# Seven block products for a sequence transform, with the feature transform behind them

## The chip, the cores and the metric

One core of a Trainium2 chip runs the kernel. The metric is the device time of one execution in microseconds (us); the kernel before takes 1925.48 us, the median of three runs.

The core's engines are TensorE (PE in the profile; PEld is its loading of weights), VectorE (DVE), ScalarE (ACT) and GpSimd (POOL); SP issues most transfers. TensorE writes into eight PSUM banks of 128 x 512 floats; TensorE's operands come from SBUF.

## The reference, cut to what matters

Four layers on an x of 2048 rows (the sequence) by 512 columns (the features): a spectral layer, an attention layer, and the same two again.

```
def _A_ref(x, dft_seq_re, dft_seq_im, dft_hid_re, dft_hid_im):
    a = jnp.einsum("bsd,ed->bse", x, dft_hid_re)
    b = jnp.einsum("bsd,ed->bse", x, dft_hid_im)
    return jnp.einsum("ts,bse->bte", dft_seq_re, a) - jnp.einsum("ts,bse->bte", dft_seq_im, b)

x = x + _A_ref(_layernorm(x), ...)      # spectral: both transforms, real part
x = x + _B_ref(_layernorm(x), ...)      # segmented attention with a memory, 32 heads, 4 segments
x = x + _A_ref(_layernorm(x), ...)
x = x + _B_ref(_layernorm(x), ...)
```

All is float32. The sequence matrices are 2048 x 2048, the feature matrices 512 x 512. Either transform may be done first; both kernels do the sequence first.

## The kernel before

Each float32 operand of a large product is split into a hi part (rounded to fp32r, TensorE's fast float format) and a lo part (the rest): ScalarE makes hi (L83), VectorE or GpSimd makes lo = source - hi (L85). `matmul3` (L91, matmuls at L71 of the wrapper) then issues three matmuls, hi hi, hi lo and lo hi.

A spectral layer (`place_spectral`) has these parts. `normalise(i)` loads one of 16 row tiles (128 x 512), takes its statistics, makes xn (L143) and splits it into `xh[i]`: hi on ScalarE, lo on GpSimd. `load_c(p, pc)` loads two row tiles' worth of the sequence matrix for a block of 512 output rows and splits it into chi and clo, 1024 wide. `contract(p)`, p from 0 to 7 (four column blocks `tcn` of 512 rows, real and imaginary), runs over the 16 row tiles: four PSUM banks u, one for each 128 features, 12 matmuls a tile. At the end of a pass the four banks are split into ut. `hidden(tcn)` multiplies them with the feature matrices wdt, eight steps of three matmuls for each of 16 row tiles of output y, and `finish` adds the residual xr (L148, VectorE) and stores the row. The hidden steps of three column blocks lie between the steps of later passes; those of the fourth lie one to a slot at the start of the attention.

The attention layer (`place_attention`) transposes the normalised rows, makes q, k and v (pqk, pvv), writes pieces of q and k to DRAM and reads them back as stacks, takes row maxima of the scores (`natural_max`, L418 on VectorE), the scores again for the softmax (sT, L483 and L484 on ScalarE), the product with the values into `pv_bank`, and the output projection (po).

The order is written out by hand. `place(order, generator, slots)` puts each step of a generator in a numbered slot; the slots are then run through in order, within a slot by `order`. Matmuls keep this order on TensorE; the other engines' order is planned from it, each engine then running its list in order. The sequence transform takes two slots for a row tile, 256 slots in all; the attention begins (`b1`, `b2`) at slot 286 of its spectral layer, and its first projections, stacks and maxima lie up to 60 slots ahead of that.

Buffers: tag `w` has 16 pairs (xh, later the attention's weights), `chi` and `clo` three each, `craw` two, `ut` and `wd` eight each. PSUM has seven rotating banks and `pv_bank` for good.

Of the kernel before, what the change touches and what calls it, by code (L numbers as in the profile page):

```python
# [37 lines left out]
MROWS = 3  # L38
MCOPIES = 5
VW = DH + 1  # L40
CP = 2
URGENT = 150


@with_exitstack
def spectral_infini_kernel(
# [58 lines left out]
    def pair(name, tag, bufs, dtype=F32R):  # L105
        return sb.tile([P, 2, 512], dtype, name=name, tag=tag, bufs=bufs)
# [10 lines left out]
        split(w[:, 0], w[:, 1], raw)  # L117
        yield

    def row_stats(xt):  # L120
        st = sb.tile([P, 6], F32, name="st", bufs=2)
        V.bn_stats(st, xt)
        mv = sb.tile([P, 2], F32, name="mv", bufs=3)
        V.bn_aggr(mv, st)
        ve = sb.tile([P, 1], F32, name="ve", bufs=3)
        V.tensor_scalar_add(ve, mv[:, 1:2], EPS)  # L126
        r = sb.tile([P, 1], F32, name="r", bufs=3)
        G.tensor_tensor(out=r, in0=ve, in1=half_neg, op=ALU.pow)  # L128
        return mv, ve, r
# [6 lines left out]
    def layernorm(xt, mv, ve, r):  # L136
        t = sb.tile([P, 1], F32, name="rt", bufs=2)
        V.scalar_tensor_tensor(t, r, r, ve, op0=ALU.mult, op1=ALU.mult)
        V.tensor_scalar(t, t, -0.5, 1.5, op0=ALU.mult, op1=ALU.add)  # L139
        rr = sb.tile([P, 1], F32, name="rr", bufs=2)  # L140
        V.tensor_mul(rr, r, t)
        xn = sb.tile([P, D], F32, name="xn", bufs=2)
        V.tensor_scalar(xn, xt, mv[:, 0:1], rr, op0=ALU.subtract, op1=ALU.mult)  # L143
        return xn
# [20 lines left out]
    def run_from(t, n, step=1):  # L165
        return range(t, t + n * step, step)

    def place_spectral(x_in, x_out, t0, ln_at, resident):
        xh, cs, wdt, u = {}, {}, {}, {}
        NP = 2 * TC  # L170

        EARLY = 12 if t0 else 0
        PRE = 4 if t0 else 0
        pre = []

        def kt(p, i):
            return t0 + 2 * (p * NT + i) - (4 if p == 0 and i < EARLY else 0)

        def preload():
            pre.append(sb.tile([P, PRE, CP, 512], F32, name="cpre", tag="xT", bufs=1))  # L180
            for pc in range(PRE):
                for c in range(CP):
                    nc.sync.dma_start(pre[0][:, pc, c], ct[0, 0, pc, :, c])
                    yield

        def normalise(i):
            leads = i == 0 and t0 == 0
            xt = None if i in LAST and t0 else load_rows(x_in[i])
            yield
            xt = resident[i] if xt is None else xt  # L190
            with behind_first(0 < i < 3):
                stats = row_stats(xt)
            yield
            xn = layernorm(xt, *stats)
# [6 lines left out]
        def load_c(p, pc):  # L201
            if p == 0 and pc < PRE:
                raw = pre[0][:, pc]
            else:
                raw = pair("craw", "craw", 2, F32)
                nc.sync.dma_start(raw, ct[p % 2, p // 2, pc])
            yield
            hi, lo = pair("chi", "chi", 3), pair("clo", "clo", 3)
            with behind_first(p == 0 and pc == 0):
                split(hi, lo, raw)  # L210
            cs[p, pc] = (hi, lo)
            yield

        def contract(p):
            us = [bank(f"u{d}") for d in range(DT)]
            for i in range(NT):
                cp = cs[p, i // CP]
                for d in range(DT):
                    matmul3(
                        us[d],  # L220
                        lambda h: xh[i][:, h, d * P : (d + 1) * P],
                        lambda h: cp[h][:, i % CP],
                        i == 0,
                        i == NT - 1,
                    )
                if i < NT - 1:
                    yield
            for d in range(DT):
                ut = pair("ut", "ut", 8)
                split(ut[:, 0], ut[:, 1], us[d], 1.0 if p % 2 == 0 else -1.0)  # L230
                u[p, d] = ut
            yield

        def hidden(tcn):
            for tt in range(LT):
                ps = bank("y")
                xr = load_rows(x_in[tcn * LT + tt], "xr")
                for c in range(2):
                    for d in range(DT):
                        ut, w = u[2 * tcn + c, d], wdt[c, d]  # L240
                        matmul3(
                            ps,
                            lambda h: ut[:, h, tt * P : (tt + 1) * P],
                            lambda h: w[:, h, :],
                            (c, d) == (0, 0),
                            (c, d) == (1, DT - 1),
                        )
                        if (c, d) != (1, DT - 1):
                            yield
                finish(ps, xr, x_out, tcn * LT + tt)  # L250
                yield

        for i in range(NT):
            t = ln_at(i)
            place(3, normalise(i), [t, t, t] if i == 0 and t0 == 0 else [t - (8 if i < 12 else 4), t - 3, t])
        if PRE:
            place(2.5, preload(), [kt(0, 0) - 46 + 10 * k + c for k in range(PRE) for c in (0, 2)])
        for p in range(NP):
            for pc in range(NT // CP):
                t = kt(p, pc * CP)  # L260
                place(3, load_c(p, pc), [t - 10, t - (2 if p == 0 and pc < PRE else 4)])
            place(2, contract(p), [kt(p, i) for i in range(NT)])
        for k in range(2 * DT):
            c, d = k // DT, k % DT
            t = kt(1, k)
            place(3, load_split(wdt, (c, d), wd[c, d], "wdt", "wd", 8), [t - 3, t])
        nh = 2 * DT * LT
        for tcn in range(TC):
            if tcn < TC - 1:
                at = [kt(2 * tcn + 2, 2) + 3 * k // 4 for k in range(nh)]  # L270
            else:
                at = run_from(kt(NP, 0), nh)
            place(4, hidden(tcn), at)

    def place_attention(x_in, x_out, t0, w_at, out_at, resident):
        ws, xT, vt, o_nat, state, scr, phi, stacks, maxima, outs = ({} for _ in range(10))
        k_stacks = []

        def prep(s, i):
            xt = load_rows(x_in[s * LT + i])  # L280
# [181 lines left out]
        def softmax_values(s, g, u):  # L462
# [83 lines left out]
                ev(h // 2, third)  # L546

            def last():
                pb = pv_bank
# [159 lines left out]
        def outproj_split(s, i):  # L709
# [23 lines left out]
            finish(ps, xr, x_out, s * LT + i, tag="wd", bufs=8)  # L733
            yield

        def alloc_out(s):
            o_nat[s] = [pair("onat", "wd", 8, F32) for _ in range(LT // 2)]
            yield
# [20 lines left out]
        for k in range(4 * DT):  # L759
            n, d = "qkvo"[k // DT], k % DT  # L760
            src = rows((wq, wk, wv, wo)[k // DT], d)
            place(3, load_split(ws, (n, d), src, f"w{n}", "w", 16), [w_at(k) - 3, w_at(k)])
        for n in range(NSEG * USEG):
# [49 lines left out]
    ]  # L813

    resident = {}
    LB, LEAD = NSEG * NG * (HG // HU) * 10, 46
    a1 = 0
    b1 = a1 + 240 + LEAD
    a2 = b1 + LB + 1
    b2 = a2 + 240 + LEAD  # L820

    def w_at(b):
        return lambda k: b - 52 + 2 * k if k < 12 else b - 14 + 2 * (k - 12)

    place_spectral(x_tiles, mids[0], a1, lambda i: a1 - 6 + 2 * i - (30 if i == 0 else 0), resident)
    place_attention(
        mids[0], mids[1], b1, w_at(b1), lambda k: b1 + LB + 8 + k // 2, resident
    )
# [88 lines left out]
```

## Time and profile before

| | |
|---|---|
| median of three runs | 1925.48 us (1923.19 to 1926.77) |
| profiled execution | 1927.09 us, of which the span of the profile is 1925.3 |
| TensorE busy | 1841.9 us, 96% |
| VectorE, ScalarE, GpSimd busy | 57%, 50%, 27% |
| mean transfer rate | 120 GB/s |
| matmuls of the sequence transforms (u) | 3072, of 10528 |
| first matmul; last of the first transform; last y of it | 9.4; 440; 492 us |
| first and last u of the second transform; last y of it | 963; 1397; 1448 us |

Rows of groups give the code line, the engine, the operation, the tile written and those read, the shape, the count, then busy us and mean ns of one, then the idle time before them and what ended it. A tile's own rows give least, median and greatest duration in ns instead, then the first and the last start. Tables of stretches give for each stretch its length, then busy us (and instructions) of PE, PEld, DVE, ACT and POOL, the granted TensorE clock, the share of the DMA engines and GB/s. Time lines give the start, the duration, and what ran; equal neighbours are merged with a count. Instructions of one engine are pipelined, so one can start about 0.1 us before its predecessor's end.

### The profile page before, as it was taken

How to read it: one execution, taken by the hardware profiler on the slowest of the kernel's cores; microseconds unless marked ns; L12 is line 12 of the kernel's file. 1: busy time of each engine (PE TensorE's matmuls, PEld its weight loads, DVE VectorE, ACT ScalarE, POOL GpSimd, SP SyncE). 2: the span in 40 equal slices, each digit the busy share in tenths (PEclk: the TensorE clock that was granted, in tenths of full speed). 3: DMA queues.
4: the chain of work that ended last, by engine and by line, in shares of the span. 5: the costliest groups of instructions: out<-in, count | busy, mean ns of one | idle time of the engine just before them, and what ended most of it. 6: DMA issues, size and time to landing. Idle time of an engine off the chain costs nothing. (4 is left out here: it accounts for less than half of the span.)

```text
span 1925.3 us, 30850 instructions
## 1 busy us (share of the span) xinstructions
PE 1841.9 (96%) x10528; PEld 1330.9 (69%) x10528; DVE 1092.2 (57%) x3665; ACT 961.1 (50%) x2026; POOL 515.1 (27%) x854
## 2 busy tenths in 40 slices
PE   7899999999989999998899999999999999999998
PEld 5788888887656666665478888888875566666654
DVE  8522222254777977878744222222557778777674
ACT  3321212132677778687733122121427877777775
POOL 5100000003443435355420000000134434444442
PEclk9999999999999999999999999999999999999999
DMA  5523222345443433435224322222454324344331
GB/s 177 162 88 110 92 95 98 104 151 159 134 125 109 152 114 128 138 117 166 73 98 142 99 98 94 95 97 94 158 170 138 127 93 151 114 130 139 110 123 45
DMA packets 122542, 231.41 MB, mean 120 GB/s; under 512 B 14352, under 2 KB 63504, under 8 KB 122384
## 3 DMA queue, kind: packets, MB, share of 16 engines
q1 hardware_dynamic: 119120, 228.65, 36.8%
q8 instruction: 83, 1.36, 0.3%
q10 hardware_dynamic: 3264, 0.79, 0.2%
q14 instruction: 75, 0.61, 0.1%
HBM read 161.50 MB, written 67.11 MB: 119 GB/s over the span
## 5 line engine op out<-in xcount | busy, mean ns | idle before, releaser
L71 PE MATMUL u<-chi,xh 128*128 128x512 f32 x2048 | 650.2, 391 | 15.1 <-ACT chi L83 9.4
L418 DVE CUSTOM_DVE_ANT_0 junk<-nat,mask 128x512 bf16<-128x512 f32 (+3 forms) x1024 | 496.4, 485 | 176.0 <-PE nat L71 156.1
L71 PEld LDWEIGHTS u<-chi,xh 128*128 128x128 f32 x2048 | 385.7, 188 | 97.5 <-ACT chi L83 9.4
L71 PE MATMUL u<-clo,xh 128*128 128x512 f32 x1024 | 400.0, 391 | 3.1 <-DVE clo L85 3.1
L83 ACT ACTIVATE chi<-craw 128x1024 fp32r<-128x1024 f32 x124 | 131.3, 1059 | 530.0 <-PE u L71 512.7
L85 DVE TENSOR_TENSOR clo<-craw,chi 128x1024 fp32r<-128x1024 f32 x124 | 153.2, 1236 | 421.2 <-ACT chi L83 420.7
L484 ACT ACTIVATE pT<-sT 128x512 f32<-128x512 f32 x640 | 369.2, 599 | 15.4 <-ACT sT L483 3.0
L487 POOL TENSOR_SCALAR_AFFINE_SELECT pT<-pT 128x256 f32<-128x256 f32 (+1 forms) x448 | 197.8, 455 | 416.4 <-ACT pT L484 346.5
L71 PE MATMUL sT<-stkq,stkk 99*128 99x256 bf16 (+3 forms) x1024 | 247.7, 305 | 14.1 <-DVE mx L418 4.6
L71 PE MATMUL nat<-stkk,stkq 96*128 96x512 bf16 (+3 forms) x1024 | 245.3, 300 | 15.5 <-DVE mx L418 12.4
L128 POOL TENSOR_TENSOR r<-ve,half_neg 128x1 f32<-128x1 f32 x64 | 39.1, 611 | 815.9 <-DVE ve L126 806.9
L483 ACT ACTIVATE sT<-sT 128x256 f32<-128x256 f32 (+1 forms) x640 | 207.8, 335 | 55.0 <-PE sT L71 48.6
L71 PEld LDWEIGHTS u<-clo,xh 128*128 128x128 f32 x1024 | 192.9, 188 | 44.3 <-DVE clo L85 4.5
L71 PE MATMUL y<-wdt,ut 128*128 128x512 f32 x768 | 196.5, 390 | 0.0
L71 PEld LDWEIGHTS <-stkk 99*128 99x128 bf16 x1024 | 82.4, 98 | 139.6 <-issue 122.5
L71 PE MATMUL pv_bank<-pT,vt 128*17 128x128 f32 (+3 forms) x2048 | 163.9, 449 | 8.4 <-POOL pT L487 8.4
L71 PEld LDWEIGHTS y<-wdt,ut 128*128 128x128 f32 x768 | 144.0, 188 | 30.0
L71 PEld LDWEIGHTS <-stkq 96*128 96x128 bf16 x1024 | 94.2, 99 | 69.1 <-issue 29.6
L71 PE MATMUL po<-wo,oh 128*128 128x512 f32 x384 | 125.6, 445 | 8.1 <-DVE rt L139 2.5
L71 PE MATMUL pqk<-xT,wq 128*128 128x512 f32 x384 | 131.8, 453 | 0.7 <-DVE mx L418 0.5
L71 PEld LDWEIGHTS pv_bank<-pT,vt 128*17 128x17 f32 x2048 | 58.9, 99 | 101.8 <-issue 79.5
L71 PE MATMUL pvv<-wv,xT 128*128 128x512 f32 x384 | 126.1, 436 | 2.3 <-DVE mx L418 1.6
(105 smaller groups left out, 1990.3 us busy)
## 6 DMA issues: line engine op xcount, KB each, us to landing
craw<-in_ct SPq DMA_DIRECT2D x124, 512.0 KB
stkq<-scrq SPq DMA_DIRECT2D x64, 384.0 KB
stkk<-scrk SPq DMA_DIRECT2D x64, 384.0 KB
mid<-xo SPq DMA_DIRECT2D x48, 256.0 KB
scrq<-parts SPq DMA_DIRECT2D x32, 384.0 KB
scrk<-parts SPq DMA_DIRECT2D x32, 384.0 KB
xr<-mid SPq DMA_DIRECT2D x48, 256.0 KB
xt<-mid SPq DMA_DIRECT2D x40, 256.0 KB
```

Source lines behind the costliest of these rows:

```text
L71: return tc.keep_in_program_order(op(*args, **kwargs))
L83: A.activation(hi, src, AF.Copy, scale=scale)
L85: lo_engine.tensor_tensor(out=lo, in0=src, in1=hi.bitcast(F32), op=ALU.subtract)
L128: G.tensor_tensor(out=r, in0=ve, in1=half_neg, op=ALU.pow)
L418: V.tensor_tensor_reduce(junk[:, :n], src, mask[:, 512 - n :], 1.0, 3e38, ALU.add, ALU.min, dst,)
L483: A.activation(blocks, blocks, AF.Relu)
L484: A.activation(dst, ps, AF.Exp, scale=-SCALE)
L487: G.affine_select(blocks, blocks, pattern=[[0, n] for n in blocks.shape[1:-1]] + [[1, P]], compare_op=ALU.is_ge, fill=0.0, base=0, channel ...
```

## The change

The sequence transform of one column block, features by (real, imaginary) over the 2048 rows, is written as a 2 x 2 block product: 256 features by 1024 rows, 1024 rows by 512 columns. It is then done with seven block products in Strassen's form in place of eight.

The left factors are differences and sums of the row tiles k and k + 8. Three belong to the sums ("A21+A22", "A11+A12", "A11+A22"), four to the differences. The differences come first for all four column blocks (32 slots each; k from 0 to 7, four products to a k), then the sums for all four (24 slots each). `normalise` makes one feature half minus the other on GpSimd (256 wide) and splits the result into xa, so the mean and the scale of each row are kept; `add_rows(k)` reads rows k and k + 8 again beside the fourth block of differences, normalises them again, adds them (whole rows on VectorE, 256 wide on GpSimd) and splits them into xb and xs, which take the places of xa.

The right factors are made in `make_right`: of the four blocks of the matrix, two sums on VectorE and two subtractions on GpSimd for a k of the differences, one sum on GpSimd for a k of the sums; each result is split 512 wide on ScalarE and VectorE. The raw blocks lie in a ring in the place of xT and in craw.

Each product takes two PSUM banks over its eight k. At its end ScalarE copies it, or VectorE adds it, into the block sums c (`TERMS`). The feature transform of the whole layer then runs in one stretch behind both groups, two or three steps to a slot, and splits c for each output row tile (`split_u`); the feature matrices are loaded just ahead of it into craw, chi and clo. PSUM has eight rotating banks; the attention takes its value bank from them and clears it at its start. A spectral layer has 224 slots and 70 up to the attention's start.

The core of the diff:

```diff
-    pv_bank = psum.tile([P, 512], F32, name="pv_bank", tag="pv", bufs=1)
-    V.memset(pv_bank, 0.0)
-        return psum.tile(list(shape), dtype, name=name, tag="bank", bufs=7)
+        return psum.tile(list(shape), dtype, name=name, tag="bank", bufs=8)
...
-            xh[i] = pair("xh", "w", 16)
-            lo = split(xh[i][:, 0], xh[i][:, 1], xn, lo_engine=V if leads else G, hi_engine=V if leads else A)
+            plain, diff = xn[:, : D // 2], xn[:, D // 2 :]
+            if i >= HALF:
+                plain, diff = diff, plain
+            (V if leads else G).tensor_tensor(out=diff, in0=diff, in1=plain, op=ALU.subtract)
+            xa[i] = pair("xa", "w", 16)
+            lo = split(xa[i][:, 0], xa[i][:, 1], xn, lo_engine=V if leads else G, hi_engine=V if leads else A)
...
+        def add_rows(k):
+            xt = [load_rows(x_in[i]) for i in (k, k + HALF)]
+            yield
+            xn = [sb.tile([P, D], F32, name="xn", bufs=2) for _ in xt]
+            for n, i in enumerate((k, k + HALF)):
+                normal(i, xt[n], xn[n])
+            cross = sb.tile([P, 512], F32, name="rem", bufs=1)[:, : D // 2]
+            G.tensor_tensor(out=cross, in0=xn[0][:, : D // 2], in1=xn[1][:, D // 2 :], op=ALU.add)
+            V.tensor_tensor(out=xn[0], in0=xn[0], in1=xn[1], op=ALU.add)
+            xb[k] = pair("xb", "w", 16)
+            split(xb[k][:, 0], xb[k][:, 1], xn[0])
...
+            split(half[:, 0], half[:, 1], cross)
...
+        def make_right(tcn, k, names):
...
+                if name in ("A21+A22", "A11+A12"):
+                    src = b[0, 0] if name == "A21+A22" else b[1, 1]
+                elif name in ("A21-A11", "A12-A22", "A11+A22"):
+                    src = sb.tile([P, 512], F32, name="praw", bufs=2)
+                    p, q = NEEDS[name]
+                    (G if name in SUMS else V).tensor_tensor(out=src, in0=b[p], in1=b[q], op=ALU.add)
+                else:
+                    p, q = NEEDS[name]
+                    src = b[p]
+                    G.tensor_tensor(out=src, in0=b[p], in1=b[q], op=ALU.subtract)
...
+                tag = ("chi", "clo")[n % 2]
+                right[tcn, name, k] = t = pair(tag, tag, 3)
+                with behind_first((tcn, k) == (0, 0)):
+                    split(t[:, 0], t[:, 1], src)
...
+        def product(tcn, name):
+            ps = [bank(f"m{m}") for m in range(2)]
+            for k in range(HALF):
+                t = right[tcn, name, k]
+                for m in range(2):
+                    matmul3(ps[m], lambda h: left(name, k, h, m), lambda h: t[:, h], k == 0, k == HALF - 1)
...
+            for m in range(2):
+                for j, op in TERMS[name]:
+                    dst = c[tcn, j][:, m]
+                    if op is None:
+                        A.activation(dst, ps[m], AF.Copy)
+                    else:
+                        V.tensor_tensor(out=dst, in0=dst, in1=ps[m], op=op)
...
+            at = [y0 + k // 2 if tcn == 0 else y0 + nh // 2 + ((tcn - 1) * nh + k) // 3 for k in range(nh)]
...
-    LB, LEAD = NSEG * NG * (HG // HU) * 10, 46
+    LB, LEAD = NSEG * NG * (HG // HU) * 10, 70
```

More of the change, by code (lines that the diff above doesn't have):

```diff
@@ L166, in run_from, with slot, normal @@
         return range(t, t + n * step, step)
+    row_mv = consts.tile([P, NT, 2], F32, name="row_mv")
+    row_r = consts.tile([P, NT], F32, name="row_r")
     def place_spectral(x_in, x_out, t0, ln_at, resident):
[L169 to L184, printed above, removed]
+        xa, xb, xs, us, wdt, c, sets, right = ({} for _ in range(8))
+        start = spectral_start(t0)
+        early = t0 > 0
+        counts = {"set": 0, "right": 0}
+        ring = []
+        def slot(tcn, name, k):
+            if name in SUMS:
+                return start + NT * LT * 2 + tcn * 3 * HALF + 3 * k + SUMS.index(name)
+            if early and tcn == 0:
+                j = DIFFS.index(name)
+                return start + 2 * HALF * (j // 2) + 2 * k + j % 2
+            return start + tcn * 4 * HALF + 4 * k + DIFFS.index(name)
+        def normal(i, xt, out):
+            V.tensor_scalar(
+                out, xt, row_mv[:, i, 0:1], row_r[:, i : i + 1], op0=ALU.subtract, op1=ALU.mult
+            )
         def normalise(i):
@@ L199, in normalise @@
             yield
[L201 to L206, printed above, removed]
-            yield
[L208 to L211, printed above, removed]
-            yield
[L214 to L218, printed above, removed]
-                    matmul3(
[L220 to L224, printed above, removed]
+        def add_rows(k):
+            xt = [load_rows(x_in[i]) for i in (k, k + HALF)]
+            yield
+            xn = [sb.tile([P, D], F32, name="xn", bufs=2) for _ in xt]
[6 more added lines that the diff above has]
+            split(xb[k][:, 0], xb[k][:, 1], xn[0])
+            if k % 2 == 0:
+                xs[k // 2] = pair("xs", "w", 16)
+            half = xs[k // 2][:, :, k % 2 * 256 : (k % 2 + 1) * 256]
+            split(half[:, 0], half[:, 1], cross)
+            yield
@@ new lines, in left, with new_set @@
+        def left(name, k, h, m):
+            src, col = {
+                "A21-A11": (xa.get(k), 2),
+                "A11": (xa.get(k), 0),
+                "A12-A22": (xa.get(k + HALF), 0),
+                "A22": (xa.get(k + HALF), 2),
+                "A21+A22": (xb.get(k), 2),
+                "A11+A12": (xb.get(k), 0),
+                "A11+A22": (xs.get(k // 2), k % 2 * 2),
+            }[name]
+            return src[:, h, (col + m) * P : (col + m + 1) * P]
+        def new_set(sums):
+            if early and counts["set"] == 2:
+                counts["set"] = 3
+            n = counts["set"]
+            counts["set"] += 1
+            if not ring:
+                ring.append(sb.tile([P, 4, 2, 512], F32, name="cring", tag="xT", bufs=1))
+            if sums:
+                return ring[0][:, n % 4], ring[0][:, n % 4]
+            if n % 3 < 2:
+                return ring[0][:, n % 3 * 2], ring[0][:, n % 3 * 2 + 1]
+            return pair("craw", "craw", 2, F32), pair("craw", "craw", 2, F32)
@@ new lines, in product, with split_u @@
+            yield
+        def split_u(tcn, tt):
+            sl = slice(tt * P, (tt + 1) * P)
+            for cc in range(2):
+                us[tcn, tt, cc] = t = pair("us", "w", 16)
+                for half in range(2):
+                    hi, lo = (
+                        t[:, h, half * 256 : (half + 1) * 256].rearrange("p (m s) -> p m s", s=P)
+                        for h in range(2)
+                    )
+                    split(hi, lo, c[tcn, (half, cc)][:, :, sl], 1.0 if cc == 0 else -1.0)
@@ L254, in place_spectral @@
             t = ln_at(i)
[L255 to L262, printed above, removed]
+            place(3, normalise(i), [t, t, t] if i == 0 and t0 == 0 else [t - (8 if i < 12 or t0 == 0 else 4), t - 3, t])
@@ new lines, in place_spectral @@
+        if early:
+            place(2.5, preload(DIFFS[:2]), [start - 46 + 7 * n for n in range(6)] + [start - 5])
+        for tcn in range(TC):
+            groups = [DIFFS[:2], DIFFS[2:]] if early and tcn == 0 else [DIFFS]
+            for names in groups + [SUMS]:
+                for k in range(HALF):
+                    t = slot(tcn, names[0], k)
+                    pre = early and tcn == 0 and k < 2 and names == DIFFS[:2]
+                    at = t - 4 if pre else t - 8 if len(names) == 2 else t - 11
+                    if names == SUMS and tcn == 0 or names == DIFFS and tcn == 1 and early:
+                        at = max(at, slot(tcn, names[0], 0) - 7)
+                    place(3, make_right(tcn, k, names), [at, t - 4])
+                for name in names:
+                    place(2, product(tcn, name), [slot(tcn, name, k) for k in range(HALF)])
@@ L263, in place_spectral @@
+        for k in range(HALF):
+            t = start + 3 * 4 * HALF + 4 * k
+            place(3, add_rows(k), [t + 4, t + 8])
+        y0 = spectral_end(t0)
         for k in range(2 * DT):
-            c, d = k // DT, k % DT
-            t = kt(1, k)
-            place(3, load_split(wdt, (c, d), wd[c, d], "wdt", "wd", 8), [t - 3, t])
+            cc, d = k // DT, k % DT
+            tag = "craw" if k < 2 else ("chi", "clo")[k % 2]
+            t = y0 - 12 + 2 * k if k < 2 else y0 - 3 + (k - 2) // 2
+            place(3.5, load_split(wdt, (cc, d), wd[cc, d], "wdt", tag, 2 if k < 2 else 3), [t - 5, t])
@@ L267, in place_spectral @@
         nh = 2 * DT * LT
         for tcn in range(TC):
[L269 to L272, printed above, removed]
+            at = [y0 + k // 2 if tcn == 0 else y0 + nh // 2 + ((tcn - 1) * nh + k) // 3 for k in range(nh)]
+            for tt in range(LT):
+                place(3.7, split_u(tcn, tt), [at[tt * 2 * DT] - 4])
             place(4, hidden(tcn), at)
@@ L734, in outproj_split, with alloc_pv @@
             yield
+        def alloc_pv():
+            pv_banks.append(bank("pv_bank"))
+            V.memset(pv_banks[0], 0.0)
+            yield
         def alloc_out(s):
```

115 lines of the change are left out of this document (89 added, 26 removed).

## The prediction

> **What bounds the kernel now.** I read the page first, then the groups of instructions, then a table of stretches, then the time lines of VectorE and GpSimd where TensorE waits.
>
> ```profile
> span 1925.3 us, 30850 instructions
> PE 1841.9 (96%) x10528; PEld 1330.9 (69%) x10528; DVE 1092.2 (57%) x3665; ACT 961.1 (50%) x2026; POOL 515.1 (27%) x854
> PE   7899999999989999998899999999999999999998
> DVE  8522222254777977878744222222557778777674
> L71 PE MATMUL u<-chi,xh 128*128 128x512 f32 x2048 | 650.2, 391 | 15.1 <-ACT chi L83 9.4
> L71 PE MATMUL u<-clo,xh 128*128 128x512 f32 x1024 | 400.0, 391 | 3.1 <-DVE clo L85 3.1
> ...
> 0.00:25.00 25.00, 12.24 (x44) 9.05 (x45) 18.41 (x55) 7.83 (x10) 12.94 (x28) 1.00 0.61 200
> 25.00:50.00 25.00, 23.52 (x103) 18.70 (x101) 23.57 (x62) 8.03 (x12) 16.39 (x17) 1.00 0.47 148
> 50.00:75.00 25.00, 20.96 (x83) 16.51 (x84) 18.96 (x28) 13.18 (x20) 5.57 (x4) 0.93 0.70 221
> 100.00:200.00 100.00, 100.00 (x443) 82.81 (x442) 26.33 (x27) 20.35 (x23) 0.00 (x0) 1.00 0.30 95
> ```
>
> TensorE bounds it, and most purely in the two sequence transforms: between 100 and 200 us it has no idle time and issues 443 matmuls, 0.2257 us each (the 391 ns of a row is one pipelined matmul from end to end). VectorE has 26 us of work in those 100 and GpSimd none. The opposite holds in the first 75 us: VectorE is full there (23.57 of 25), GpSimd has 16.39 of 25, and TensorE waits. Why VectorE and GpSimd do not simply work side by side is seen in their time lines; these are VectorE's rows, then GpSimd's.
>
> ```profile
> 38.81 0.54 DVE L143 TENSOR_SCALAR xn<-xt,mv,rr 128x512 f32<-128x512 f32 x1
> 39.26 0.18 DVE L124 BATCH_NORM_AGGREGATE mv<-st 128x2 f32<-128x6 f32 x1
> 39.39 2.32 DVE L85 TENSOR_TENSOR clo<-craw,chi 128x1024 fp32r<-128x1024 f32 x1
> 41.70 1.18 DVE L141 TENSOR_TENSOR rr<-r,rt 128x1 f32<-128x1 f32 x1
> ...
> 55.42 0.69 DVE L85 TENSOR_TENSOR wdt<-raw,wdt 128x512 fp32r<-128x512 f32 x1
> 56.02 1.22 DVE L85 TENSOR_TENSOR clo<-craw,chi 128x1024 fp32r<-128x1024 f32 x1
> 57.16 3.58 DVE L85 TENSOR_TENSOR wdt<-raw,wdt 128x512 fp32r<-128x512 f32 x4
> ```
>
> ```profile
> 39.34 3.52 POOL L85 TENSOR_TENSOR xh<-xn,xh 128x512 fp32r<-128x512 f32 x2 [0.71 <-ACT xh L83]
> 56.25 2.13 POOL L85 TENSOR_TENSOR xh<-xn,xh 128x512 fp32r<-128x512 f32 x1 [1.35 <-ACT xh L83]
> ```
>
> ```profile
> L85 DVE TENSOR_TENSOR clo<-craw,chi x124: 1207/1226/2322, 9.4 to 1379.3; 128x1024 fp32r<-128x1024 f32 x124
> L85 POOL TENSOR_TENSOR xh<-xn,xh x31: 1255/1285/2268, 16.9 to 1014.5; 128x512 fp32r<-128x512 f32 x31
> L85 DVE TENSOR_TENSOR wdt<-raw,wdt x16: 652/684/1777, 53.1 to 1019.2; 128x512 fp32r<-128x512 f32 x16
> ...
> L138 DVE SCALAR_TENSOR_TENSOR rt<-r,ve x64: 207/220/1223, 5.3 to 1633.6; 128x1 f32<-128x1 f32 x64
> L141 DVE TENSOR_TENSOR rr<-r,rt x64: 144/159/1224, 5.8 to 1638.8; 128x1 f32<-128x1 f32 x64
> ...
> L128 POOL TENSOR_TENSOR r<-ve,half_neg x64: 547/550/1677, 4.8 to 1630.6; 128x1 f32<-128x1 f32 x64
> ```
>
> The last fence has least, median and greatest duration in ns. A subtraction on VectorE with both inputs in SBUF and a subtraction on GpSimd exclude each other. The clo that normally takes 1.226 us takes 2.32 when a GpSimd op started 0.05 us ahead; the next GpSimd op waits for that clo (two take 3.52 us, not 2 x 1.285), and then rr, a one-column op, takes 1.18 us. The prices: GpSimd holds VectorE off for 58.38 (56.25 + 2.13) - 57.24 (56.02 + 1.22) = 1.14 us per 512-wide subtraction; VectorE's pitch for one of 512 is 56.02 - 55.42 = 0.60, for one of 1024 it is 57.16 - 56.02 = 1.14, for xn 39.26 - 38.81 = 0.45.
>
> Does that add up over a stretch? VectorE's, then GpSimd's rows for 10 to 58 us:
>
> ```profile
> L85 DVE TENSOR_TENSOR clo<-craw,chi 128x1024 fp32r<-128x1024 f32 x8 | 10.9, 1358 | 0.6 <-ACT chi L83 0.4 <-issue 0.2
> L143 DVE TENSOR_SCALAR xn<-xt,mv,rr 128x512 f32<-128x512 f32 x15 | 10.0, 664 | 2.1 <-POOL xh L85 1.7
> L141 DVE TENSOR_TENSOR rr<-r,rt 128x1 f32<-128x1 f32 x15 | 7.4, 491 | 0.1
> L138 DVE SCALAR_TENSOR_TENSOR rt<-r,ve 128x1 f32<-128x1 f32 x15 | 5.1, 343 | 1.5 <-POOL r L128 1.1
> L85 DVE TENSOR_TENSOR wdt<-raw,wdt 128x512 fp32r<-128x512 f32 x3 | 3.1, 1049 | 0.0
> ```
>
> ```profile
> L85 POOL TENSOR_TENSOR xh<-xn,xh 128x512 fp32r<-128x512 f32 x15 | 21.6, 1449 | 9.4 <-ACT xh L83 9.4
> L128 POOL TENSOR_TENSOR r<-ve,half_neg 128x1 f32<-128x1 f32 x15 | 11.2, 746 | 10.5 <-DVE mv L124 4.7 <-DVE rt L138 2.5 <-DVE ve L126 1.7
> ```
>
> GpSimd 15 x 1.14 + 15 x 0.46 (r, my estimate of what of its 0.55 excludes VectorE) = 24.0; VectorE 8 x 1.14 + 3 x 0.60 + 15 x 0.45 + 15 x 0.2 (rr and rt, 0.159 + 0.220 less a tenth each for the overlap of neighbours) = 20.7. Together 44.7 us of the 48. So in that stretch the sum of both engines, not the longer one, set the time.
>
> **The change part by part** (us against the profiled execution, 1927.1 with a span of 1925.3, 1.6 above the median).
>
> *Fewer matmuls.* A transform goes from 8 passes x 16 x 4 x 3 = 1536 matmuls to 4 x 7 x 8 x 2 x 3 = 1344. 2 x 192 x 0.2257 = -86.7, where TensorE is the bound. Everything else is what the new additions cost.
>
> *What one step of the first group needs.* Per column block and k: four right tiles, 24 matmuls, 5.42 us of TensorE. VectorE makes two additions and four lo, all 512 wide with two SBUF inputs, 6 x 0.60 = 3.60; GpSimd two subtractions, 2 x 1.14 = 2.28. Serial: 5.88, or 0.46 over TensorE. The four additions from PSUM per eight k (a row of the old kernel with one PSUM input has 0.69, xo below) add 4 x 0.60 / 8 = 0.30, half of it hidden behind GpSimd. I take 0.6 per k. Six right tiles of buffer (three chi, three clo) are 8 us ahead at most and cannot carry it. Bounds: 0, if the subtractions fall into VectorE's gaps, up to 1.26 (6 x 0.684 + 2 x 1.285 - 5.42). There are 8 groups of 8 k; the very first has its own term: 56 x 0.6 = +34.
>
> *The very first group.* Besides its rights, each k needs two new rows. Excluding work per k: GpSimd 2 x (0.46 + 0.59 + 1.14) + 2.28 = 6.66, where 0.59 is the new 256-wide difference (0.73 us on a line through the 128-wide row below and the 1.285, less the same 0.14); VectorE 2 x (0.45 + 0.2) + 3.60 = 4.90. 8 x 11.56 = 92, from 10 us on: done at 102. The old kernel has done as many matmuls (one pass) at 65.3, when its first ut is read. +36; the lower bound is GpSimd alone, 8 x (2 x (0.55 + 0.73 + 1.285) + 2 x 1.285) = 62, +7.
>
> ```profile
> L591 POOL TENSOR_TENSOR onat<-onat,otmp 128x128 f32<-128x128 f32 x96 | 43.5, 469 | 33.4 <-DVE otmp L590 32.6 <-PE nat L71 0.2
> L83 ACT ACTIVATE ut<-u x4: 578/593/608, 65.3 to 66.7; 128x512 fp32r<-128x512 f32 x4
> L148 DVE TENSOR_TENSOR xo<-y,xr x32: 679/688/692, 129.8 to 1448.0; 128x512 f32<-128x512 f32 x32
> ```
>
> *Rows read again for the sums.* Each of eight steps beside the fourth column block adds on VectorE 2 x 0.45 + 0.60 + 0.60 + 0.33 (256 wide) = 2.43 and on GpSimd 0.59, 3.02 in all, on top of a port that is already behind. The last two run beside the second group, which has room (below). 6 x 3.02 = 18 per transform, +36; lower bound 5.7 each (VectorE alone, 3.60 + 0.30 + 2.43 - 5.42 = 0.9 per k).
>
> *Second group.* 18 matmuls, 4.06 us per k, against 3 x 0.60 + 1.14 = 2.94 and 12 x 0.60 / 8 = 0.90 from PSUM: fits. 0; if its 12 PSUM additions come in a lump, 1 to 2 us for each of eight.
>
> *Second transform's late rows.* Four rows still come after its start: 4 x (2.19 + 0.65) = 11.4 against the 48 matmuls of the out-projection there, 10.8: +4 with what GpSimd already has; bounds 0 and 10.
>
> *Feature-axis stretch.* As many matmuls as before, so 0 for itself; per row tile eight 256-wide splits and one finish beside 5.4 us. At its start VectorE has 8 wdt lo, 12 PSUM additions and two rows' splits, 8 x 0.60 + 12 x 0.60 + 8 x 0.35 = 14.8, in slots that give TensorE 10.8: +4 each, +8.
>
> *Ramp into attention.* The feature transform used to run one step a slot up to the first softmax, and now ends 22 slots ahead of it.
>
> ```profile
> 460.00:500.00 40.00, 38.16 (x186) 26.08 (x185) 32.38 (x128) 14.61 (x31) 13.24 (x19) 1.00 0.39 128
> 1415.00:1455.00 40.00, 39.02 (x191) 26.90 (x189) 30.58 (x126) 13.94 (x29) 12.72 (x18) 1.00 0.42 137
> ```
>
> Without 22 x 3 x 0.2257 = 14.9 of filler, TensorE has 23 us of work in the 460 to 500 stretch and VectorE 30 (32.4 less three finishes): the stretch plus the moved filler is 45, not 40. +5 each, +10; bounds 0 and 20.
>
> *Transfers and banks.* The first group reads 1 MB per 5.4 us, 194 GB/s; the table has 200 at a share of 0.61 and 221 at 0.70, so it fits: 0. SP has two issues per k where it had one per two steps, and a load whose ring set is busy holds up the row loads behind it; three sets are 16 us ahead. Four products fill all eight banks, so a product waits for its predecessor's reading: two ACT copies (0.593 each) against three slots of 1.35 us, hidden unless ACT's queue is late. The value bank's memset is one op per layer: 0.
>
> Sum: -86.7 + 34 + 36 + 36 + 4 + 8 + 10 = +41, 1968 for the profiled execution and **1967** for the median.
>
> A rule weighed: the Trainium skill, SBUF — State Buffer, section "Who interferes with whom", says that a VectorE op with two SBUF inputs and a GpSimd op that reads SBUF block each other fully, and its terms call the pair held "for the full instruction". The trace agrees on the blocking; on the length it has 1.14 of 1.285 us and 0.60 of 0.684, so by the page the time would be that of the third rival.
>
> **The rivals.**
>
> 1. *The pairing does not bind outside the start* (faster). If GpSimd's subtractions find gaps, VectorE's 3.9 us per k is under TensorE's 5.42. The terms become 0 (groups), +7 (start), 2 x 5.7, 0, +8, +10: -86.7 + 36 = -50, **1876**. For it: in steady state VectorE would have gaps. Against it: the sum of 44.7 in 48 us, and no buffer to shift work. It decides at 5.42 us per k. Chance 0.20.
> 2. *It binds only where rows are made* (start and sums), and the groups hide it: 1927 - 86.7 + 36 + 36 + 4 + 8 + 10 = **1934**, or a little under with a shorter ramp. Chance 0.15, half of it within 0.2% or below.
> 3. *Each op holds the pair for its whole row* (slower still): 1.26 + 0.15 per k is +79, the start 8 x (2 x (0.55 + 0.73 + 1.285 + 0.54 + 0.38) + 6.67) = 109, +52, the sums 6 x 3.6 x 2 = +43: +109, **2036**. Against it: by whole rows (1.285, 0.55, 1.226, 0.684, 0.54, 0.38) the 10 to 58 us stretch would hold 53 us of work, more than its length. Chance 0.08.
> 4. *The change leaves the matmul count as it is*: excluded by the loops.
>
> **How the numbers follow.** The forecast, 1935 to 2005 by its bounds, has 0.57. The range 1875 to 2015 takes in rivals 1 and 2 and leaves about 0.2 out. 0.2% (4 us) is about what these runs can tell from no change. Faster: 0.20 + 0.06 + 0.01; same: 0.06; slower: the rest, 0.67.
>
> **What would show it.** Right: in the changed profile 192 matmuls fewer per transform; the first group done near 100 us; in the column blocks TensorE idle by a tenth and more, released by VectorE's or GpSimd's work, with GpSimd subtractions or VectorE lo well above 1.285 and 0.684; the fourth block worst; the second group without idle time. Wrong: TensorE at 440 per 100 us in the first group too (rival 1), or idle time that transfers or banks end.

## The result, and the profile after

The changed kernel takes 1996.78 us against 1925.95 (medians of four): 1.0374 times as long, interval 1.0356 to 1.0392, or 71 us more. The forecast was 1967 with a range from 1875 to 2015. In the spans of the two profiled executions the difference is 1994.8 - 1925.3 = 69.5 us.

From the page of the changed kernel:

```profile
span 1994.8 us, 32632 instructions
PE 1816.2 (91%) x10144; PEld 1268.4 (64%) x10144; DVE 1591.5 (80%) x4387; ACT 1148.9 (58%) x2506; POOL 879.6 (44%) x1093
PE   4699889999889999898878998999998899999998
DVE  7899999865787787877858999989457878777684
L114 DVE TENSOR_TENSOR chi<-praw,chi 128x512 fp32r<-128x512 f32 x160 | 185.8, 1161 | 16.2 <-ACT chi L112 16.2
L314 POOL TENSOR_TENSOR cring<-cring 128x512 f32<-128x512 f32 x88 | 138.8, 1578 | 109.7 <-DVE praw L310 95.2
```

TensorE issues 384 matmuls fewer, as the loops say, and its share falls from 96 to 91%: it waits longer than it saves. VectorE gained 499 us of busy time. How much of that is work is told by the durations: the lo of a right tile, 0.684 us undisturbed, takes 1.161 us on average where its source came from praw, and GpSimd's subtraction 1.578 us, not 1.285. Both numbers contain waiting; the profile counts an instruction that is held off as busy.

A table of stretches, each cut where the next group's first matmul starts: of the first transform the first, second and fourth group of differences and the first two blocks of sums, then the ramp into the attention, then the first group of the second transform:

```profile
0.00:105.60 105.60, 65.27 (x193) 45.62 (x194) 86.58 (x169) 33.03 (x56) 78.16 (x81) 0.85 0.50 159
105.60:156.50 50.90, 46.92 (x193) 34.99 (x192) 50.35 (x59) 23.67 (x41) 26.27 (x17) 1.00 0.55 172
206.40:269.80 63.40, 50.85 (x194) 35.60 (x192) 61.49 (x78) 25.74 (x50) 33.92 (x21) 0.97 0.52 161
269.80:305.80 36.00, 35.30 (x145) 27.97 (x145) 33.14 (x47) 21.89 (x41) 16.37 (x11) 0.95 0.54 176
305.80:339.60 33.80, 32.90 (x145) 26.95 (x144) 31.95 (x45) 17.27 (x31) 13.22 (x8) 1.00 0.38 125
507.40:535.00 27.60, 22.39 (x100) 14.72 (x99) 22.74 (x92) 7.00 (x13) 11.43 (x13) 0.88 0.57 179
...
1013.00:1088.60 75.60, 63.77 (x297) 48.92 (x295) 57.51 (x94) 29.78 (x57) 40.22 (x38) 0.95 0.54 185
```

At 0.2257 us a matmul the 192 matmuls of a difference group would take 43.3 us and the 144 of a block of sums 32.5. They take 50.9 (second difference group), 63.4 (fourth, beside the added rows), 36.0 (first sums) and 33.8 (later sums). In the second group VectorE is busy 50.35 of 50.90 us with 59 instructions, 0.85 us each, though none of them has more than about 0.7 us where nothing holds it off. Its time line, and GpSimd's, 133 to 139 us:

```profile
132.89 0.68 DVE L114 TENSOR_TENSOR clo<-cring,clo 128x512 fp32r<-128x512 f32 x1
133.50 1.51 DVE L213 TENSOR_SCALAR xn<-xt,row_mv,row_r 128x512 f32<-128x512 f32 x1
...
136.25 0.69 DVE L114 TENSOR_TENSOR clo<-cring,clo 128x512 fp32r<-128x512 f32 x1
136.85 1.78 DVE L114 TENSOR_TENSOR chi<-praw,chi 128x512 fp32r<-128x512 f32 x1
138.67 0.69 DVE L310 TENSOR_TENSOR praw<-craw 128x512 f32<-128x512 f32 x1
```

```profile
133.10 1.61 POOL L314 TENSOR_TENSOR cring<-cring 128x512 f32<-128x512 f32 x1 [1.28 <-DVE praw L310]
136.46 1.62 POOL L314 TENSOR_TENSOR cring<-cring 128x512 f32<-128x512 f32 x1 [1.74 <-DVE praw L310]
```

Each GpSimd subtraction starts under a lo, waits for its end (136.25 + 0.69 = 136.94) and runs to 138.08, 1.14 us later. The next VectorE op waits for that: the lo at 136.85 ends 0.55 us behind it, and the normalisation of a row at 133.50 takes 1.51 us. It is the alternation of the old kernel's start, now in every k. The second thing to see is L213 at 133 us: a row for the sums is normalised here, in the second group, although its place in the written order is beside the fourth. VectorE's list is planned, and the plan put some of this work here.

Where no row comes between, as through most of the third group, the alternation has a fixed beat:

```profile
176.51 0.69 DVE L310 TENSOR_TENSOR praw<-craw 128x512 f32<-128x512 f32 x1
177.12 0.69 DVE L114 TENSOR_TENSOR clo<-cring,clo 128x512 fp32r<-128x512 f32 x1
177.72 1.78 DVE L114 TENSOR_TENSOR chi<-praw,chi 128x512 fp32r<-128x512 f32 x1
179.54 0.69 DVE L310 TENSOR_TENSOR praw<-craw 128x512 f32<-128x512 f32 x1
```

One GpSimd subtraction and three VectorE ops, half of a k, take 179.54 - 176.51 = 3.03 us: 1.14 for GpSimd, and 1.89 for VectorE, not 3 x 0.60. Undisturbed neighbours on VectorE start about 0.08 us before their predecessor's end (177.12 against 177.20); the op behind the held-off lo starts 0.04 us after it (179.54 against 179.50).

The ledger of the 69.5 us, from the first and last starts of u, m, y and sT in both traces (time beyond 0.2257 us a matmul, against the same in the old kernel; for the fourth groups the part without added rows is taken from the run that leaves these out, below):

| step | predicted | measured |
|---|---|---|
| 384 matmuls fewer | -86.7 | -86.7 |
| very first group with the start | +36 | +33.9 |
| six later difference groups, without added rows | +29 | +43 |
| second transform's first group, with its late rows | +9 | +9.6 |
| rows read again for the sums | +36 | +32 |
| sums, beyond the first block | 0 | +8 |
| start of the feature stretch | +8 | +6.6 |
| ramps, and the attentions behind them | +10 | +24 |
| sum | +41 | +70 |

### The profile page after: what moved, and what is told of

It is laid out like the page before. It is cut to its first block, busy times and chain, and to the rows that moved or that the text cites. A ratio compares the mean times of both kernels' runs of the same rounds, so it can differ in the third digit from the quotient of the medians.

```text
span 1994.8 us, 32632 instructions
## 1 busy us (share of the span) xinstructions
PE 1816.2 (91%) x10144; PEld 1268.4 (64%) x10144; DVE 1591.5 (80%) x4387; ACT 1148.9 (58%) x2506; POOL 879.6 (44%) x1093
## 5 line engine op out<-in xcount | busy, mean ns | idle before, releaser
L100 PE MATMUL m<-chi,xa 128*128 128x512 f32 x768 | 227.7, 420 | 56.7 <-DVE chi L114 21.1
L100 PE MATMUL m<-clo,xa 128*128 128x512 f32 x768 | 215.3, 414 | 21.3 <-DVE c L350 11.5
L100 PEld LDWEIGHTS m<-chi,xa 128*128 128x128 f32 x768 | 146.1, 198 | 117.3 <-DVE chi L114 47.7
L114 DVE TENSOR_TENSOR chi<-praw,chi 128x512 fp32r<-128x512 f32 x160 | 185.8, 1161 | 16.2 <-ACT chi L112 16.2
L100 PEld LDWEIGHTS m<-clo,xa 128*128 128x128 f32 x768 | 149.7, 199 | 67.1 <-DVE clo L114 17.2
L314 POOL TENSOR_TENSOR cring<-cring 128x512 f32<-128x512 f32 x88 | 138.8, 1578 | 109.7 <-DVE praw L310 95.2
L100 PE MATMUL y<-wdt,us 128*128 128x512 f32 x768 | 181.3, 391 | 3.3 <-DVE wdt L114 3.3
L310 POOL TENSOR_TENSOR praw<-cring 128x512 f32<-128x512 f32 x64 | 109.1, 1707 | 154.3 <-DVE clo L114 82.5
L100 PEld LDWEIGHTS y<-wdt,us 128*128 128x128 f32 x768 | 143.4, 188 | 33.7 <-DVE wdt L114 4.1
L114 DVE TENSOR_TENSOR clo<-cring,clo 128x512 fp32r<-128x512 f32 x152 | 135.8, 893 | 9.7 <-ACT clo L112 8.7
```

The lines of the kernel that those rows point to most:

```text
L100: return tc.keep_in_program_order(op(*args, **kwargs))
L114: lo_engine.tensor_tensor(out=lo, in0=src, in1=hi.bitcast(F32), op=ALU.subtract)
L310: (G if name in SUMS else V).tensor_tensor(out=src, in0=b[p], in1=b[q], op=ALU.add)
L314: G.tensor_tensor(out=src, in0=b[p], in1=b[q], op=ALU.subtract)
```

## The experiments

**Subtractions on VectorE.** The rival to the exclusion is that VectorE simply has too much to do.

```diff
-                    G.tensor_tensor(out=src, in0=b[p], in1=b[q], op=ALU.subtract)
+                    V.tensor_tensor(out=src, in0=b[p], in1=b[q], op=ALU.subtract)
```

> The two subtractions per k of the difference groups go from GpSimd to VectorE; all else as in the changed kernel (1997 us). Theory 1, the two engines exclude each other: VectorE then needs 8 x 0.60 + 0.30 = 5.1 us per k, 5.7 with the rows added for the sums spread over the groups, and GpSimd no longer holds it off. Second and third group 50 -> 46 us, fourth 63 -> 52, first (done at 105.6) -> 98; about 1945 to 1955 us. Theory 2, VectorE is simply full (its row is 98% busy in these groups): two more ops of 0.60 us per k on the full engine make it slower, 64 x 1.2 = +77, about 2070 us.

1954.4 us, against 1996.8. The second group of this run:

```profile
104.20:148.00 43.80, 43.80 (x194) 35.95 (x193) 43.72 (x78) 24.66 (x42) 0.00 (x0) 1.00 0.67 205
```

VectorE, "98% busy", did 78 instructions in 43.7 us where it had done 59 in 50.4. Theory 2 falls: the full engine took on 19 more and finished earlier. The fourth group falls to 49.2 us, and the first block of sums rises from 36.0 to 41.4. The first group did not follow (done at 104.2, expected 98). How long GpSimd waits there for VectorE, 25 to 87 us, in the changed kernel and in this run (in all, how often, the longest):

```profile
POOL r L154 <- DVE ve L152: 4.5, 5, 0.9
```

```profile
POOL r L154 <- DVE ve L152: 16.5, 5, 3.3
```

GpSimd, with less to do, now stands idle longer until VectorE has made the statistics (ve) of the new rows.

**No subtractions.** The same line is left out.

> Leaves out the two subtractions per k of the difference groups (a part of the computation), so GpSimd has none there; VectorE has exactly the work it had. Theory 1 (exclusion): VectorE's own work per k is 3.9 us, 4.5 with the added rows, under TensorE's 5.42, so second and third group fall from 50 to about 44 us, the fourth from 63 to about 48, the first is done near 88; about 1915 us in all. Theory 2 (VectorE full of its own work): nothing changes, 1992 to 2000 us.

1914.0 us, as theory 1 has it. The first two groups of this run:

```profile
12.50:87.30 74.80, 58.59 (x193) 42.29 (x194) 70.19 (x158) 29.87 (x53) 47.77 (x45) 0.89 0.57 184
87.30:130.80 43.50, 43.50 (x194) 36.02 (x193) 38.14 (x66) 24.94 (x43) 1.72 (x1) 1.00 0.71 223
```

TensorE has no idle time in the second, and transfers ran at 223 GB/s, so they were not what bound it. That is also the price of the two subtractions: 43.5 to 50.9 us in this group.

**All sums and differences on VectorE.**

```diff
-                    (G if name in SUMS else V).tensor_tensor(out=src, in0=b[p], in1=b[q], op=ALU.add)
+                    V.tensor_tensor(out=src, in0=b[p], in1=b[q], op=ALU.add)
...
-            G.tensor_tensor(out=cross, ...)
+            V.tensor_tensor(out=cross, ...)
```

> As the run with the subtractions on VectorE, and also the sum of the second group and the 256-wide sum of the added rows on VectorE. Theory 1: VectorE needs 4 x 0.60 + 0.90 = 3.3 us per k of the second group, under 4.06, so nothing is lost there; the added rows get 0.26 us each cheaper; 0 to 6 us under the run with the subtractions alone. The stall of 1.3 us at the start of each second-group block stays, as it comes from 12 additions from PSUM in a row on VectorE. Theory 2: 64 x 0.6 + 16 x 0.33 = +44 us over that run.

1938.0 us, 16 below the run before, more than the 0 to 6 expected: the fourth difference group of the first transform takes 46.6 instead of 49.2, the first block of sums 39.4 instead of 41.4, and the second transform gains 7. A later block of sums:

```profile
276.90:310.80 33.90, 33.02 (x146) 26.96 (x145) 30.03 (x53) 17.33 (x31) 0.00 (x0) 1.00 0.39 125
```

These blocks stay at 33.9 without a single GpSimd instruction, so it is not GpSimd that costs 1.3 us there.

**Added rows left out.**

```diff
-                "A21+A22": (xb.get(k), 2),
+                "A21+A22": (xa.get(k), 2),
...
-            place(3, add_rows(k), [t + 4, t + 8])
+            pass
```

> Leaves out a part of the computation: the rows are not read again, normalised again, added and split; the sums' products take xa in place of xb and xs. Theory: each of the eight steps costs 3.02 us of the pair's time in each transform while the pair is behind, 24 each; the fourth difference block falls from 63 us to about 49 and the second and third, into which some of this work was planned, from 50 to 47 or 48; 1950 to 1960 us. Rival: the fourth block is late because of its transfers or buffers; it stays above 58 us and the time above 1985.

1969.1 us, 28 less; 1950 to 1960 was expected. The third and the fourth group and the first sums:

```profile
154.30:204.30 50.00, 47.16 (x194) 34.98 (x192) 49.55 (x53) 23.83 (x41) 25.70 (x16) 1.00 0.55 169
204.30:255.00 50.70, 47.06 (x193) 35.00 (x192) 49.66 (x55) 25.41 (x45) 25.38 (x16) 1.00 0.55 168
255.00:287.70 32.70, 32.70 (x146) 27.06 (x145) 26.26 (x34) 17.06 (x29) 12.77 (x9) 1.00 0.46 141
```

The fourth group is now like the third, so the added rows made it late, and 3.3 us of the first sums as well. The rows' own loads and buffers went with them here; that these are not what counts is seen below, where the added rows are loaded as before, normalised on ScalarE, and the fourth group takes 43.7. The third group did not get shorter: without any row work a k costs 50.0 / 8 = 6.25 us. The gain is 32 in these stretches and partly given back: the feature stretch of this run takes 102.5 us, not 100.1, twice; why is not shown.

**The lump of additions.** In the changed kernel a block of sums ends with this on VectorE, and TensorE waits:

```profile
337.09 7.26 DVE L350 TENSOR_TENSOR c<-c,m 128x512 f32<-128x512 f32 x12
344.26 0.69 DVE L114 TENSOR_TENSOR clo<-cring,clo 128x512 fp32r<-128x512 f32 x1
...
345.00 1.43 PE L100 MATMUL m<-clo,xb 128*128 128x512 f32 x5 [0.90 <-DVE clo L114]
```

The first edit gave the additions of each product slots behind the block.

```diff
+                    if name in SUMS:
+                        end = slot(tcn, SUMS[-1], HALF - 1) + 1 + 2 * SUMS.index(name)
+                        place(3.2, gen, [end, end + 1])
```

> The changed kernel, with the 12 additions from PSUM at the end of each block of the sums put one pair to a slot behind the next block's right tiles, not in one lump ahead of them. Theory: the second group loses only because of that lump (one stall of about 1.3 us at each block's start); three blocks of each transform then take 32.6 us, not 33.8, the first one or two less than 36; 1986 to 1991 us, against 1997. Rival: GpSimd's sum and VectorE's lo bind there too; then the blocks stay at 33.8 and the time at 1995 to 1999.

2008.9 us, 12 slower. Both expectations missed: the later blocks take 35.4 to 37.2 us. What TensorE waits for in one of them, and the feature stretch of this run:

```profile
PE m L100 <- DVE c L350: 2.4, 2, 1.6
```

```profile
415.30:512.20 96.90, 96.90 (x437) 80.21 (x436) 52.10 (x113) 27.78 (x63) 10.80 (x12) 1.00 0.51 161
```

The wait is for the additions themselves: three products hold six of eight banks, so the next block's second and third product wait for banks that are now emptied late. The lump costs right tiles, spreading it costs banks. Only the third product's banks are not needed soon. The feature stretch gains: without the last block's lump ahead of it, it runs without idle time in 96.9 us, where the changed kernel has 100.1.

**Added rows on ScalarE, with the same spreading**, on the all-on-VectorE version.

```diff
-            V.tensor_scalar(out, xt, row_mv[:, i, 0:1], row_r[:, i : i + 1], op0=ALU.subtract, op1=ALU.mult)
+            A.activation(out, xt, AF.Identity, bias=row_nb[:, i : i + 1], scale=row_r[:, i : i + 1])
```

> As the run with every sum and difference of the right tiles on VectorE, with two more edits: the additions from PSUM spread over the next block's slots, and the added rows normalised on ScalarE (scale and bias per row), which takes 2 x 0.45 us per step from VectorE. Theory: 8 to 10 us less for the lumps and 5 to 14 us less for the rows than that run's 1938: 1914 to 1926 us, level with the kernel before or a little faster. If VectorE is not what binds any more there, it stays above 1930.

1937.2 us where 1914 to 1926 was expected, no gain in all (1.0058 of before, 1.0039 to 1.0078; 1.0063 without the two edits), from two effects: the fourth group falls from 46.6 to 43.7 and the first sums from 39.4 to 34.3, and the spread blocks rise to 35.5 to 37.

**The version that follows.** All sums on VectorE, the added rows and the first transform's new rows normalised on ScalarE, and of a block's additions only those of the third product put off, by three slots.

```diff
+                    if name == SUMS[-1]:
+                        end = slot(tcn, name, HALF - 1) + 3
+                        place(3.2, gen, [end, end + 1])
```

> As the run with every sum and difference of the right tiles on VectorE (1938 us), with the added rows and, in the first transform, the new rows normalised on ScalarE, and of the 12 additions from PSUM at a block's end only the third product's four put off by three slots (no bank waits for those: its two are the next but one to be taken). Theory (banks made the spread version slow, the pair's total makes the first group slow): blocks of sums at 32.6 to 33.8 us, difference groups at 43.5, first group 91 -> 84; 1912 to 1922 us, under the kernel before (1926). If the blocks stay at 35 and the first group at 90: 1932 to 1938.

1903.5 us, 0.9887 of the kernel before (0.9850 to 0.9923), 93 us under the changed kernel and some 9 below what was expected. Its first, second and fourth group, a block of sums and the feature stretch:

```profile
14.10:98.60 84.50, 60.72 (x192) 42.32 (x193) 72.62 (x174) 41.10 (x69) 49.56 (x45) 0.84 0.51 156
98.60:142.10 43.50, 43.50 (x193) 36.05 (x192) 43.32 (x77) 26.00 (x44) 0.00 (x0) 1.00 0.70 217
185.60:229.50 43.90, 43.82 (x193) 35.98 (x193) 43.72 (x77) 31.00 (x54) 0.00 (x0) 1.00 0.64 199
263.80:296.50 32.70, 32.70 (x146) 27.08 (x145) 29.89 (x53) 17.00 (x31) 0.00 (x0) 1.00 0.41 129
361.70:458.60 96.90, 96.90 (x436) 80.23 (x435) 52.18 (x113) 27.90 (x63) 10.77 (x12) 1.00 0.51 161
```

In the groups where GpSimd does nothing, the transform runs at TensorE's pitch, with VectorE over 99% busy. The blocks of sums are at TensorE's pitch too, so it was the lump that cost 1.3 us a block. The seven-product form gains here, but 25 us and not 87: the first group and the ramps remain.

**The ramp in the old kernel.**

```diff
-                at = run_from(kt(NP, 0), nh)
+                at = [kt(NP, 0) + k // 3 for k in range(nh)]
```

> The kernel before, with one edit: the feature-transform steps of the fourth column block lie three to a slot right behind the sequence transform instead of one to a slot up to the attention's start. If the ramp of the attention needs that filler, both ramps lose what the changed kernel lost there: 12 to 15 us each, 1950 to 1956 us (5 each and 1936 by the prediction's term). If the changed kernel lost it for another reason (its late weights and splits), 1923 to 1930 us.

1945.7 us, 1.0094 of before (1.0058 to 1.0129), 18 us more for two ramps: the missing filler alone costs 9 each, between the prediction's 5 and the 12 to 15 expected after the result. Its stretch from the last y steps to the first softmax:

```profile
470.00:497.30 27.30, 22.21 (x80) 13.34 (x78) 22.21 (x87) 5.07 (x9) 7.86 (x10) 0.75 0.40 126
```

TensorE starts 80 matmuls in 27 us, at a granted clock of 0.75, and VectorE is not full either (22.21 of 27.30 us).

**Statistics held back.** In the changed kernel's ramp one wait stands out (520 to 530 us): the first transposed maxima wait for VectorE.

```profile
PE mT L100 <- DVE mparts L583: 5.2, 1, 5.2
```

```diff
+            with tc.issue_after(anchor[-1].ins) if s == 1 else nullcontext():
                 stats = row_stats(xt)
```

> The changed kernel (1997 us) with the statistics of the attention's second segment held behind the maxima of the first units. Theory: 4 to 6 us less per ramp, 1985 to 1989 us; else 1995 to 1999.

2000.0 us, no gain (1.0376 of before, as the changed kernel's 1.0374). The first ramp did get shorter; the first and last sT of the first attention, in the changed kernel and in this one:

```profile
L100 PE MATMUL sT<-stkq,stkk x512: 217/326/634, 533.5 to 1016.2; 99*128 99x256 bf16 x43, 99*128 99x128 bf16 x43, 99*128 99x512 bf16 x43, 99*128 99x384 bf16 x42
```

```profile
L100 PE MATMUL sT<-stkq,stkk x512: 217/322/634, 528.2 to 1019.2; 99*128 99x256 bf16 x43, 99*128 99x128 bf16 x43, 99*128 99x512 bf16 x43, 99*128 99x384 bf16 x42
```

From the last y to the first sT it is 528.2 - 508.5 = 19.7 us instead of 533.5 - 507.4 = 26.1, and then the attention takes 491.0 instead of 482.7: by the edit the statistics are done later, among the maxima of later units. The wait was real, but what its removal gave was lost again in the attention; where in it, and whether to the statistics, is not shown. The same edit on the version of 1903.5:

> As the run before it in this list, and the statistics of the attention's second segment are held behind the maxima of the first units on VectorE's list. Theory: in the ramp TensorE waits for VectorE's maxima (5.2 us for the first transposed maxima), among which six rows' statistics of about 1 us each were planned; without them the ramp is 4 to 6 us shorter, twice: 8 to 12 us less. If the maxima wait for scores or transfers, nothing changes.

1908.9 us, 0.9904 of before (0.9881 to 0.9926): no gain either.

**The value bank alone, in the old kernel.** Eight rotating banks and the attention's own clearing.

> The kernel before, with the third part of the change alone: eight rotating banks, of which the attention takes its value bank at its start and clears it. Theory: it costs nothing, 1923 to 1930 us. Rival: its bank waits or the clearing stand in the attention's ramp, 1 to 3 us each, 1928 to 1934 us.

1926.3 us, 0.9998 of before (0.9985 to 1.0011): nothing, as predicted.

## Why the prediction was right, and where its sizes were off

- *What decides.* Right: VectorE's sums, lo and row normalisations and GpSimd's subtractions exclude each other, and the sum of both, not the longer one, sets the pace. Shown by taking the GpSimd op away (50.9 to 43.5 us) and by moving it to the engine that looked full (43.8). Rivals 1 and 2 are out: the groups do not hide it. Rival 3 is too: a k without rows costs 6.25 us, not 6.83.
- *Difference groups, +0.6 per k.* Too small: 50.0 us is 0.83 per k over TensorE. The step that was mis-sized is "Serial: 5.88": it has all six VectorE ops at the undisturbed pitch of 0.60 us. The beat in the trace is 3.03 for half a k, 6.06 for a whole one, as the op behind a held-off lo does not overlap with it. That is 0.18 per k, or 9 of the 14 us that the six groups of the ledger are over their term. "Half of it hidden behind GpSimd" came out nearer: 6.06 and the 0.30 of the additions from PSUM are 6.36, and 6.25 was measured. The trace agrees: at 109.07 us a GpSimd subtraction runs for 1.30 us beside two additions from PSUM of 0.67 us each, and neither engine holds the other off. But of the 12 additions in the second to fourth group of the first transform only 4 meet a subtraction.
- *The very first group.* Forecast done at 102, done at 105.6: +40 for +36 against the 65.3 us that the prediction took from the old kernel. The ledger's +33.9 sets against it 6 us more, which the old kernel loses later in its first transform and the prediction left out. The agreement is partly luck. The same sum gave 84 us, 8.6 less, for the run with its subtractions on VectorE; measured are 91.0, 0.5 less. The sum has no term for the statistics of two new rows per k, which VectorE makes and GpSimd waits for; in that run these waits grow from 4.5 to 16.5 us. Without the subtractions the group takes 74.8, as the sum has it (8 x 2.28 = 18 less), and with the rows' normalisation on ScalarE 84.5. How much the granted clock of 0.85 adds in this group is not shown; TensorE is idle there for 40 of the 105.6 us.
- *Added rows.* 32 for 36. Right in size, wrong in place: part was planned into the second difference group, and 8 us fell into the first block of sums of the two transforms, which I had said has room.
- *Second group (the sums), 0.* Wrong, by the bound that the prediction named: the 12 additions come in a lump, 1.3 us for each of three blocks, twice. So one of its signs, a second group without idle time, did not come; with four of the 12 put off the blocks are at 32.4 to 32.7.
- *Feature stretch.* +6.6 for +8, and for the reason given, the lump of work at its start: one gap of 1.65 us on wdt and slower steps behind it, all gone (96.9 us) where the additions are spread.
- *Ramps, +5 each.* The term most undersized: +24 for +10 with what the attentions took. Comparing VectorE's 30 us with TensorE's 23 assumes that the work is ready when VectorE is. The old kernel with the filler moved lost 9 each, 4 more than the term, with neither engine full: the 9 are shown, that waits for one another make the 4 is argued from this. The rest, some 3 each, is not explained.
- *Value bank, transfers.* 0, right: the bank alone is shown, and transfers ran at 223 GB/s where the subtractions were gone, above the 172 of the group that they would have had to bind.

## What to carry to other kernels

A scheme that saves matmuls pays in additions, and these may go to two engines that exclude each other: see in a time line which ops are held off, and add these up for both engines as one resource before comparing with TensorE. Judge a full VectorE by instructions per microsecond at undisturbed durations, not by its busy share. Moving work onto the engine that looks full can then be the cure: here all sums on VectorE, row normalisation on ScalarE and four additions of each block put off turned +71 us into -25 against the kernel before. And a wait removed in one place need not shorten the whole: the ramp's 6 us did not (2000.0 against 1996.8).

## What was not expected of the hardware

An instruction that is held off counts as busy for its whole wait (lo of 0.684 us at 1.161 on average, GpSimd's subtraction of 1.285 at 1.578), so both engines of a pair can look busy while half of it is waiting. After a wait the blocked VectorE lo takes 0.55 us to its end and the GpSimd op 1.14, the same in the changed kernel at 136 to 139 us as in the old one at 56 to 59. In the third group the two engines took strict turns, 3.03 us for three VectorE ops and one of GpSimd's. The additions with one input in PSUM took no part in it (0.67 us beside a GpSimd subtraction of 1.30).
